# A two-layer chain on one core: front weights loaded in three parts, prepared weights with a due step, spread first loads, unchained output stores

## The chip, the cores and the metric

The kernel runs on one core of a Trainium2 chip. The metric is the device time of one execution in microseconds; before the change three runs took 874.82, 874.1 and 875.6 us, with a median of 874.82 us. Engines are named as in the profile: PE is TensorE (PEld its weight loads), DVE is VectorE, ACT is ScalarE, POOL is GpSimd, and SP is the engine that issues nearly all DMAs.

## The reference

Decayed attention of 4 x 8 heads feeds a gated layer and then a second layer with a piecewise quadratic gate. Weights come as 64-bit numbers, which the chip turns into float32.

```python
scores = q @ k^T / sqrt(64)              # (4, 8, 576, 576)
x = (scores * Dmat) @ v                  # Dmat[h, i, j] = gamma_h ** (i - j) for i >= j, else 0
x = x.transpose(0, 2, 1, 3).reshape(2304, 512)
xn = x / sqrt(mean(x * x) + 1e-6) * rms_g
x = (silu(xn @ w_gate) * (xn @ w_val)) @ w_out        # first layer, 512 -> 1536 -> 512
h = x @ w_in                                          # second layer, 512 -> 2048 -> 512
g = where(h >= 1, h, where(h <= -1, 0, (h + 1) ** 2 / 4))
out = g @ w_out2                                      # (2304, 512)
```

## The kernel before, in words

The 2304 tokens are worked in three batches of 768 (`NSB = 3`, `SB = 768`). After the attention comes the first layer: 36 steps (`step_a`, line 611), twelve for each batch, one for each 128 columns of the hidden size. Then comes the second layer: for each batch a front half (`x @ w_in`) and a back half (`g @ w_out2`).

Every product of 2 x 2 blocks is done with seven block products instead of eight, and every factor is kept as a high and a low part, so that one 128-row product is three matmuls (`three`, line 562). A front unit (`front_b`, line 735) is one of eight pairs of hidden columns of a batch. It has seven products of six matmuls, in the order 0, 1, 2, 3, 4, 6, 5. The loop at line 927 puts product number i of unit p at place 2i + 7p, so that a unit begins every seven places and two units alternate; the last place of a front half is 61. At places 56, 58 and 60 the first three pieces of the back half (`back_b`, line 814) stand between front products.

The weights of a front unit are prepared in the first layer. `prepare_b` (line 362) takes one of 16 units at the steps of `PREPARE` (line 43): eight for the front and eight for the back. It loads the 64-bit weights from `in_wb`, converts them (`convert`, line 284), makes sums (`wsum`), splits high from low into the one buffer `prep`, and stores 1792 KB to DRAM, to `wfd` for the front and `wod` for the back.

In the second layer unit q reads its weights from `wt0` or `wt1` (q even or odd). `load_wf` (line 701) loads them in two transfers: products 0 to 2 (768 KB) and products 3 to 6 (1024 KB). The first transfer for unit q + 2 is put after product 2 of unit q, when its place in the buffer is free, and the second after the last product of unit q.

`load_piece` (line 786) loads 512 KB of back weights from `wod` into a ring of six (`wback`). The ring shares its memory with `prep`. In batch 0 six of these loads are put at places 48 to 58 of the front half; afterwards each piece that is done loads one further on.

A result of the back half is added, transposed into a half of `o`, and stored by four DMAs of 96 KB (`store_out`, line 800). For the last result, which goes through a part of `plain`, two of the four are issued by ACT and two by SP.

What is written is not issued in that order. All engine calls go through `Plan` (line 46). `take` (line 98) records each with the earlier ones that it must follow, found from the overlap of the memory they touch; for DRAM that is the span from first to last element. `issue` (line 135) then works backwards through the list for a due time of each operation from costs of its own, and forwards for an order on every engine: of the operations that could start, the one due first. TensorE takes the first in the written order. So a due time sets how early an operation stands on VectorE, ScalarE and SP. `later_than` holds an operation back until a given one is done. On the chip each engine then runs its own list in order.

```python
for j, w, q in self.seen.get(name, []):            # take: who must come before
    over = r[0] < q[1] and q[0] < r[1] and r[2] < q[3] and q[2] < r[3]
    if over and (write or w or ...):
        before.add(j)
...
work = {2 * i + 7 * p: run for p in range(NPB) for i, run in enumerate(front_b(b * NPB + p))}
```

Of the kernel before, what the change touches and what calls it, by code (L numbers as in the profile page):

```python
# [36 lines left out]
EPS = 1e-6  # L37
WARM = 16
STAGE = 3
ATT = 6  # L40
FRONT, BACK = 0, 1
UNITS = [(p, kind) for p in range(NPB) for kind in (FRONT, BACK)]
# [3 lines left out]
class Plan:  # L46
# [8 lines left out]

    def __init__(self, nc):
        self.ops, self.seen, self.floor = [], {}, None
        for name in ("tensor", "vector", "scalar", "gpsimd", "sync"):
            setattr(self, name, Taker(self, name, getattr(nc, name)))

# [37 lines left out]
    def take(self, engine, real, method, args, kwargs):  # L98
        whole = lambda a: a[tuple(slice(None) for _ in a.shape)] if hasattr(a, "tag") else a
        args = [whole(a) for a in args]  # L100
        kwargs = {k: whole(a) for k, a in kwargs.items()}
        is_ap = lambda a: hasattr(a, "dep_tracking_offset")
        out = args[0] if args else kwargs["out"]
        ins = [a for k, a in kwargs.items() if k != "out" and is_ap(a)]
        if method == "matmul":
            ins = [kwargs["lhsT"], kwargs["rhs"]]
        i = len(self.ops)
        before = set()
        for ap, write in [(a, False) for a in ins] + [(out, True)]:
            name, *r = self.region(ap)  # L110
            kept = []
            for j, w, q in self.seen.get(name, []):
                over = r[0] < q[1] and q[0] < r[1] and r[2] < q[3] and q[2] < r[3]
                if over and (write or w or ap.space == PSUM and self.ops[j][0] != engine):
                    before.add(j)
                inside = r[0] <= q[0] and q[1] <= r[1] and r[2] <= q[2] and q[3] <= r[3]
                if not (write and inside):
                    kept.append((j, w, q))
            kept.append((i, write, r))
            self.seen[name] = kept  # L120
        if self.floor is not None and engine != "tensor":
            before.add(self.floor)
        before.discard(i)
        call = lambda: getattr(real, method)(*args, **kwargs)  # L124
        table = {ACTF.Silu: 1, ACTF.Abs_reciprocal_sqrt: 2}.get(kwargs.get("func"), 0)
        self.ops.append((engine, call, before, self.cost(engine, method, out, ins), method == "dma_start", table))

    @contextmanager
    def later_than(self, i):
# [2 lines left out]
        yield  # L132
        self.floor = None

    def issue(self):
        ops = self.ops
        n = len(ops)
        after = [[] for _ in range(n)]
        for i, o in enumerate(ops):
            for j in o[2]:  # L140
                after[j].append(i)

        def lag(j, i):
            if ops[j][0] == ops[i][0] and not ops[j][4]:
                return self.SAME.get(ops[j][0], 0)
            return self.PE_LATENCY if ops[j][0] == "tensor" else self.LATENCY

        due = [0.0] * n
        next_pe = None
        for i in reversed(range(n)):  # L150
            late = min((due[k] - lag(i, k) for k in after[i]), default=1e12)
            if ops[i][0] == "tensor":
                if next_pe is not None:
                    late = min(late, due[next_pe])
                next_pe = i
            due[i] = late - ops[i][3]
        wait = [len(o[2]) for o in ops]
        ready = [0.0] * n
        free = {}
        queue = {}  # L160
        rank = lambda i: i if ops[i][0] == "tensor" else due[i]
        for i in range(n):
            if not wait[i]:
                queue.setdefault(ops[i][0], []).append(i)
        dma_free, order, loaded = 0.0, [], 0
        while len(order) < n:
            best = None
            for e, q in queue.items():
                if not q:
                    continue  # L170
                t0 = max(free.get(e, 650.0), min(ready[i] for i in q))
                i = min((i for i in q if ready[i] <= t0 + self.HOLD), key=rank)
                start = max(free.get(e, 650.0), ready[i])
                if best is None or start < best[0]:
                    best = start, i
            start, i = best
            e, _, _, cost, dma, table = ops[i]
            if e == "scalar" and not dma and (table or not loaded) and table != loaded:
                cost, loaded = cost + 1283, table or 1
            if e == "tensor" and start < self.COLD:  # L180
                cost *= 2
            queue[e].remove(i)
            if dma:
                free[e] = start + 60
                dma_free = max(dma_free, start) + cost - 2000
                end = dma_free + 2000
            else:
                free[e] = end = start + cost
            order.append(i)
            for k in after[i]:  # L190
                wait[k] -= 1
                ready[k] = max(ready[k], end + lag(i, k))
                if not wait[k]:
                    queue.setdefault(ops[k][0], []).append(k)
        for i in order:
            ops[i][1]()
# [10 lines left out]
@with_exitstack  # L207
def moe_chain_kernel(ctx: ExitStack, tc: tile.TileContext, att, tail, wa, wb, dmat, gq, gk, out):
    nc = Plan(tc.nc)
    one = ctx.enter_context(tc.tile_pool(name="one", bufs=1))  # L210
    psum = ctx.enter_context(tc.tile_pool(name="psum", bufs=1, space=PSUM))
    dram = ctx.enter_context(tc.tile_pool(name="dram", bufs=1, space=DRAM))
# [354 lines left out]
    def product(w, j, ps, first, last):  # L567
        w = w.rearrange("p (j w k n) -> p j w k n", j=7, w=2, k=2)
        for k in range(2):
            three(  # L570
                ps, w[:, j, 0, k], w[:, j, 1, k], xs[:, j, 0, k], xs[:, j, 1, k], first and k == 0, last and k == 1,
                skip_group_check=True,
            )
# [33 lines left out]
        return [lambda d=d, wide=wide: part(d, wide) for wide in (False, True) for d in range(KD)]  # L607

    late = []

    def step_a(s):
        b, f = divmod(s, NA)
# [17 lines left out]
        w, h = wts[s % 2], hs[s % 2]  # L630
        d, x = front_banks(s)
        product(w, 0, d, True, False)
        after(0)
        if s < NA:
            with nc.later_than(len(nc.ops) - 1):
# [52 lines left out]
            sums_x()  # L688
        if s in PREPARE:
            limit[0] = len(slots)  # L690
            with nc.later_than(len(nc.ops) - 1):
                prepare_b()
        if s + 2 >= NA:
            if s + 2 < NSB * NA:
                load_a(s + 2, 1)
            else:
                for part in range(2):
                    load_wf(s + 2 - NSB * NA, part)


    def load_wf(q, part):
        if q < NSB * NPB:
            a, b = ((0, 3), (3, 7))[part]
            nc.sync.dma_start(
                out=wts[q % 2][:, a * 4 * P:b * 4 * P].bitcast(F32), in_=wfd[q % NPB][:, a * 4 * P:b * 4 * P]
            )
# [28 lines left out]
    def front_b(q):  # L735

        b, p = divmod(q, NPB)
        w = wts[q % 2]
# [15 lines left out]
        def after_4():  # L754
            nc.scalar.copy(out=u3, in_=d)
            nc.vector.tensor_add(out=g22, in0=x, in1=u3)
            gate_b(g22, g22)

        def after_6():
            gate_b(g12, d)  # L760

        def after_5():
            nc.vector.tensor_add(out=g21, in0=x, in1=u2)
            gate_b(g21, g21)
            load_wf(q + 2, 1)
            if p % 2:
                i = p // 2
                nc.vector.tensor_add(out=two(s1, i), in0=two(h21, i), in1=two(h22, i))
                nc.vector.tensor_sub(out=two(h21, i), in0=two(h11, i), in1=two(h21, i))
# [156 lines left out]
    for b in range(NSB):  # L926
        work = {2 * i + 7 * p: run for p in range(NPB) for i, run in enumerate(front_b(b * NPB + p))}
        end = max(work)
        for i, run in enumerate(held):
            work[2 * i + 1] = run  # L930
        back = back_b(b)
        for t in (end - 5, end - 3, end - 1):
            work[t] = back.pop(0)
        for t in sorted(work):
            if b == 0 and end - 14 <= t < end - 2 and t % 2 == 0:
                with nc.later_than(len(nc.ops) - 1):
                    load_piece()
            work[t]()
        if b + 1 < NSB:
            back, held = back[:-3], back[-3:]  # L940
        for i, run in enumerate(back):
            run()
            if i == NPB and b + 1 < NSB:
                with nc.later_than(len(nc.ops) - 1):
                    load_xb(b + 1)
# [63 lines left out]
```

## Time and profile before

| | before |
|---|---|
| median of three runs | 874.82 us (874.1 to 875.6) |
| profiled execution, its own time | 874.14 us |
| its span, first to last instruction | 872.4 us |
| PE busy | 850.5 us, 97% |
| DVE busy | 674.0 us, 77% |
| ACT busy | 565.0 us, 65% |
| granted TensorE clock, mean | 0.996 |
| DMA, mean over the span | 282 GB/s |

The shares are means over stages with different limits. Attention fills about the first 95 us, the first layer goes on to about 509 us, and the second layer fills the rest. The page has one line number for nearly all instructions, L124, because `Plan` makes every call there; so groups are told apart by what they write and read. `fr`, `acc` and `at` are PSUM banks, `xall` holds the tokens, `wt` the front weights, `rounded` the back weights, hidden values and the buffer `prep`, `o` the output. `att` and `plain` are shared by many temporaries. A releaser in brackets (`<-DMA wt<-wfd`) is what ended an idle time.

### The profile page before, as it was taken

Reading aid. Unit: us, or ns where it says so; the run is one execution under the profiler, and the core shown is the slowest. Engines: PE = TensorE matmul, PEld = TensorE weight load, DVE = VectorE, ACT = ScalarE, POOL = GpSimd, SP = SyncE. Lnnn points to the kernel's source line nnn. Section 1 sums busy time; section 2 is a strip of 40 time slices with the busy share of each in tenths; the row PEclk is TensorE's granted clock in tenths of the full one; section 3 lists DMA queues with packets and bytes.
Section 4 is the critical chain, followed back from the end, with each engine's and each line's share of the span. In section 5 each row is a group of like instructions: output and inputs, shape, how many; then the busy total and the mean of one; then the engine's idle time right before and its main releaser. Section 6 shows DMA issues by size and latency. Waiting matters only on the chain.

```text
span 872.4 us, 14665 instructions
## 1 busy us (share of the span) xinstructions
PE 850.5 (97%) x5460; PEld 811.9 (93%) x5460; DVE 674.0 (77%) x1077; ACT 565.0 (65%) x1019; POOL 52.1 (6%) x64
## 2 busy tenths in 40 slices
PE   8999899999999999999999999999999999999996
PEld 7987799999999999999999998999999999999996
DVE  3789888889988887979787876876767678567854
ACT  2647788887657767877666876745467646477541
POOL 3667000000000000000000000000000000000000
PEclk9999999999999999999999999999999999999999
DMA  9996788886868889699889879899886799784795
GB/s 355 338 354 208 233 276 271 286 276 203 263 234 309 326 291 367 219 333 392 301 283 353 304 283 348 280 356 318 257 263 253 262 282 319 257 273 151 205 272 127
DMA packets 116375, 246.03 MB, mean 282 GB/s; under 512 B 28240, under 2 KB 63312, under 8 KB 111184
## 3 DMA queue, kind: packets, MB, share of 16 engines
q1 hardware_dynamic: 114640, 243.69, 81.7%
q10 hardware_dynamic: 1664, 1.40, 0.5%
q8 instruction: 43, 0.70, 0.3%
q14 instruction: 28, 0.23, 0.1%
HBM read 185.82 MB, written 59.24 MB: 281 GB/s over the span
## 4 chain that ended last, share of the span: by engine, by line
PE 83%; DMA 11%; ACT 2%; DVE 2%; issue 1%; SPq 1%; POOL 0%; DVEq 0%; ACTq 0%
PE fr L124 37%; PE acc L124 30%; PE at L124 16%; DMA wt<-wfd 5%; DMA x1d<-plain 2%; DVE plain L124 1%; DMA rounded<-wod 1%; DMA plain<-in_wa_dram 1%; DMA xall<-x2d 1%; ACT xall L124 1%; SPq L124 1%; DMA plain<-in_dmat_dram 1%; ACT rounded L124 0%; DMA att<-in_att_dram 0%; DMA wt<-wfa 0%
## 5 line engine op out<-in xcount | busy, mean ns | idle before, releaser
L124 PE MATMUL fr<-xall,wt 128*128 128x384 f32 x2016 | 400.0, 337 | 1.8 <-ACT wt L124 0.6
L124 PEld LDWEIGHTS fr<-xall,wt 128*128 128x128 f32 x2016 | 353.7, 188 | 20.8 <-ACT att L124 2.9
L124 PE MATMUL acc<-rounded 128*128 128x384 f32 (+1 forms) x1224 | 275.6, 356 | 2.7 <-ACT att L124 1.3
L124 PEld LDWEIGHTS acc<-rounded 128*128 128x128 f32 x1224 | 215.3, 188 | 10.0 <-ACT att L124 2.4
L124 DVE TENSOR_TENSOR rounded<-plain,rounded 128x768 fp32r<-128x768 f32 (+1 forms) x96 | 88.4, 924 | 40.2 <-ACT rounded L124 39.9
L124 ACT CAST rounded<-plain 128x768 fp32r<-128x768 f32 (+1 forms) x96 | 77.6, 810 | 60.7 <-PE acc L124 33.9
L124 PE MATMUL at<-rounded 128*128 128x256 f32 (+1 forms) x648 | 111.4, 299 | 1.4 <-ACT rounded L124 1.3
L124 ACT COPY att<-fr 128x384 f32<-128x384 f32 x144 | 68.8, 478 | 57.7 <-PE fr L124 56.2
L124 ACT ACTIVATE att<-att 128x384 f32<-128x384 f32 x168 | 86.4, 524 | 24.4 <-DVE att L124 23.2
L124 DVE TENSOR_TENSOR att<-fr,att 128x384 f32<-128x384 f32 x144 | 78.7, 555 | 30.2 <-PE fr L124 18.8
L124 PEld LDWEIGHTS at<-rounded 128*128 128x128 f32 x648 | 98.4, 188 | 1.9 <-ACT rounded L124 1.6
L124 DVE TENSOR_TENSOR plain<-plain 128x768 f32<-128x768 f32 (+1 forms) x88 | 72.0, 831 | 0.6
L124 DVE SCALAR_TENSOR_TENSOR plain<-att,plain 128x384 f32<-128x384 f32 x72 | 39.1, 552 | 29.2 <-ACT att L124 29.2
L124 ACT ACTIVATE att<-plain 128x384 f32<-128x384 f32 x72 | 37.9, 526 | 36.2 <-DVE plain L124 36.1
L124 DVE TENSOR_TENSOR wt<-wt 128x768 fp32r<-128x768 f32 (+1 forms) x48 | 52.1, 1088 | 10.7 <-ACT wt L124 10.0
L124 PE MATMUL acc<-xall,wt 128*128 128x384 f32 x288 | 57.9, 335 | 0.6 <-ACT att L124 0.6
L124 ACT CAST wt<-wt 128x768 fp32r<-128x768 f32 (+1 forms) x48 | 45.3, 943 | 10.8 <-DMA wt<-wfa 10.4
L124 PEld LDWEIGHTS acc<-xall,wt 128*128 128x128 f32 x288 | 50.5, 188 | 1.1 <-ACT att L124 0.9
L124 ACT ACTIVATE plain<-plain,half 128x512 uint32<-128x512 uint8 x68 | 51.5, 765 | 0.0
L124 PE MATMUL at<-xall,wt 128*128 128x384 f32 x216 | 43.8, 337 | 2.7 <-DMA wt<-wfd 2.6
L124 ACT CAST rounded<-att 128x384 fp32r<-128x384 f32 x72 | 36.3, 513 | 9.0 <-DVE att L124 9.0
L124 DVE TENSOR_TENSOR rounded<-att,rounded 128x384 fp32r<-128x384 f32 x72 | 39.2, 551 | 3.6 <-ACT rounded L124 3.3
(91 smaller groups left out, 812.8 us busy)
## 6 DMA issues: line engine op xcount, KB each, us to landing
rounded<-wod SPq DMA_DIRECT2D x84, 512.0 KB, 4.9
wt<-wfd SPq DMA_DIRECT2D x24, 1024.0 KB, 7.3
plain<-in_wa_dram SPq DMA_DIRECT2D x36, 512.0 KB, 5.0
wt<-wfd SPq DMA_DIRECT2D x24, 768.0 KB, 4.9
plain<-in_wb_dram SPq DMA_DIRECT2D x32, 512.0 KB, 6.8
wfd<-rounded SPq DMA_DIRECT2D x8, 1792.0 KB, 8.0
wod<-rounded SPq DMA_DIRECT2D x8, 1792.0 KB, 8.8
att<-in_att_dram SPq DMA_DIRECT2D x26, 512.0 KB, 6.5
```

Source lines behind the costliest of these rows:

```text
L124: call = lambda: getattr(real, method)(*args, **kwargs)
```

## The change

Four edits.

1. Each prepared unit is given a due time. The operations of a `prepare_b` at step s are noted (`wanted_by`), and at step s + 6 (`UNIT_STEPS`) they are made due no later than the last operation written then, which is a matmul of that step's first product (`due_now`). Until now they were due only by whoever reads the stored weights or needs the buffer next. The unit prepared last, at step 30, gets no such time, since there is no step 36.
2. `load_wf` has three parts instead of two: products 0 to 2 (768 KB), 3 and 4 (512 KB), 5 and 6 (512 KB). The second is put after product 4 of the unit that frees the buffer, the third after its last product.
3. The six loads of back weights in batch 0's front half are put at places 31, 36, 41, 46, 51 and 56 instead of 48 to 58.
4. `take` no longer looks for overlaps of writes to `out` (`apart`). The stores of one result cover spans of `out` that interleave, so each counted as following the one before, though they touch different rows.

```diff
@@ class Plan
         self.ops, self.seen, self.floor = [], {}, None
+        self.apart, self.wanted = None, {}
...
-            for j, w, q in self.seen.get(name, []):
+            for j, w, q in () if name == self.apart else self.seen.get(name, []):
...
+    @contextmanager
+    def wanted_by(self, got):
+
+        at = len(self.ops)
+        yield
+        got.append(range(at, len(self.ops)))
+
+    def due_now(self, got):
+
+        for part in got:
+            self.wanted.update((i, len(self.ops) - 1) for i in part)
+        got.clear()
+
...
             late = min((due[k] - lag(i, k) for k in after[i]), default=1e12)
+            if i in self.wanted:
+                late = min(late, due[self.wanted[i]])
...
     nc = Plan(tc.nc)
+    nc.apart = out.tensor.name
@@ step_a
         product(w, 0, d, True, False)
+        nc.due_now(units_b[s % UNIT_STEPS])
...
-            with nc.later_than(len(nc.ops) - 1):
+            with nc.later_than(len(nc.ops) - 1), nc.wanted_by(units_b[s % UNIT_STEPS]):
                 prepare_b()
...
-                for part in range(2):
+                for part in range(3):
                     load_wf(s + 2 - NSB * NA, part)
@@ load_wf, front_b
-            a, b = ((0, 3), (3, 7))[part]
+            a, b = ((0, 3), (3, 5), (5, 7))[part]
...
             nc.vector.tensor_add(out=g22, in0=x, in1=u3)
             gate_b(g22, g22)
+            load_wf(q + 2, 1)
...
             gate_b(g21, g21)
-            load_wf(q + 2, 1)
+            load_wf(q + 2, 2)
@@ the loop over places
-            if b == 0 and end - 14 <= t < end - 2 and t % 2 == 0:
+            if b == 0 and end - 32 <= t < end - 2 and (end - t) % 5 == 0:
                 with nc.later_than(len(nc.ops) - 1):
                     load_piece()
```

What this does to the order on the engines, at three places.

At the start of the second layer, SP's queue before. `wt0` and `wt1` are the two weight buffers; a transfer 1536 wide is the first of a unit, 2048 wide the second; `wfd` and `wod` on the left are stores of prepared weights, `x2d` stores of the first layer's result.

```order
L124 DMA wt0_64<-wfd_91 128x1536
L124 DMA x2d_94<-plain_80 128x2x256
L124 DMA wfd_91<-rounded_79 128x3584
L124 DMA x2d_94<-plain_80 128x2x256
L124 DMA wt1_65<-wfd_91 128x1536
L124 DMA wt0_64<-wfd_91 128x2048
L124 DMA x2d_94<-plain_80 128x512
L124 DMA wt0_64<-wfd_91 128x1536
L124 DMA wod_92<-rounded_79 128x3584
L124 DMA x2d_94<-plain_80 128x512
L124 DMA wt1_65<-wfd_91 128x2048
```

The same place of SP's queue now; the two later transfers of a unit are 1024 wide.

```order
L126 DMA wod_92<-rounded_79 128x3584
L126 DMA wt1_65<-wfd_91 128x1024
L126 DMA x2d_94<-plain_80 128x2x256
L126 DMA wt0_64<-wfd_91 128x1536
L126 DMA x2d_94<-plain_80 128x2x256
L126 DMA x2d_94<-plain_80 128x512
L126 DMA wt0_64<-wfd_91 128x1024
L126 DMA x2d_94<-plain_80 128x512
L126 DMA wt1_65<-wfd_91 128x1536
L126 DMA wt0_64<-wfd_91 128x1024
```

Two stores of prepared weights stood after the first transfer of unit 2 (the first row of before); now the last of them stands ahead of it (the fourth row). The unit's second transfer stands before, and its third after, the first transfer of unit 3.

TensorE in the units that follow, before (`fr` are the banks of even units, `acc3` and `at0` those of odd ones).

```order
L124 MATMUL fr1_88<-xall_63,wt0_64 128x384 x6
L124 MATMUL fr0_87<-xall_63,wt0_64 128x384 x6
L124 MATMUL fr1_88<-xall_63,wt0_64 128x384 x6
L124 MATMUL fr0_87<-xall_63,wt0_64 128x384 x6
L124 MATMUL at0_81<-xall_63,wt1_65 128x384 x6
L124 MATMUL acc3_86<-xall_63,wt1_65 128x384 x12
L124 MATMUL at0_81<-xall_63,wt1_65 128x384 x6
```

And now:

```order
L126 MATMUL at0_81<-xall_63,wt1_65 128x384 x6
L126 MATMUL fr1_88<-xall_63,wt0_64 128x384 x6
L126 MATMUL acc3_86<-xall_63,wt1_65 128x384 x6
L126 MATMUL fr0_87<-xall_63,wt0_64 128x384 x6
L126 MATMUL at0_81<-xall_63,wt1_65 128x384 x6
L126 MATMUL fr0_87<-xall_63,wt0_64 128x384 x6
L126 MATMUL acc3_86<-xall_63,wt1_65 128x384 x6
```

Before, four products of an even unit stood in a row, and then two of the odd one on the same bank, `acc3`; now the two units alternate.

Towards the end of batch 0's front half, SP's queue before (`rounded<-wod` are pieces of back weights).

```order
L124 DMA wt0_64<-wfd_91 128x1536
L124 DMA wt1_65<-wfd_91 128x2048
L124 DMA rounded_79<-wod_92 128x2x512 x2
L124 DMA wt1_65<-wfd_91 128x1536
L124 DMA wt0_64<-wfd_91 128x2048
L124 DMA rounded_79<-wod_92 128x2x512 x5
L124 DMA wt1_65<-wfd_91 128x2048
L124 DMA rounded_79<-wod_92 128x2x512 x9
```

And now:

```order
L126 DMA wt1_65<-wfd_91 128x1024
L126 DMA rounded_79<-wod_92 128x2x512 x2
L126 DMA wt0_64<-wfd_91 128x1024
L126 DMA wt1_65<-wfd_91 128x1536
L126 DMA wt0_64<-wfd_91 128x1024
L126 DMA wt1_65<-wfd_91 128x1024
L126 DMA rounded_79<-wod_92 128x2x512
L126 DMA wt0_64<-wfd_91 128x1536
L126 DMA wt1_65<-wfd_91 128x1024
L126 DMA rounded_79<-wod_92 128x2x512
L126 DMA wt0_64<-wfd_91 128x1024
L126 DMA wt1_65<-wfd_91 128x1536
```

Two pieces and then five stood close together, all but two of them behind a second transfer; now the first four stand apart, among the transfers of units 6 to 9.

The end of SP's queue before (`o` are earlier results, `plain` is the last one).

```order
L124 DMA rounded_79<-wod_92 128x2x512
L124 DMA out_0_dram<-o_68 32x12x64 x5
L124 DMA out_0_dram<-plain_80 32x12x64
L124 DMA out_0_dram<-o_68 32x12x64 x2
L124 DMA out_0_dram<-plain_80 32x12x64
```

And now:

```order
L126 DMA out_0_dram<-o_68 32x12x64 x4
L126 DMA rounded_79<-wod_92 128x2x512
L126 DMA out_0_dram<-o_68 32x12x64 x4
L126 DMA out_0_dram<-plain_80 32x12x64 x2
```

Two stores of an earlier result stood between the last two stores; now all four of that result stand ahead of both.

## Rows read from the trace of the kernel before

**Rows 1.** The page's head: span and instructions.

```profile
span 872.4 us, 14665 instructions
```

**Rows 2.** What TensorE waited for, 505 to 873 us: total us, times, longest.

```profile
PE at L124 <- DMA wt<-wfd: 2.6, 5, 0.8
PE acc L124 <- ACT att L124: 1.9, 3, 0.7
PE acc L124 <- DMA rounded<-wod: 1.3, 1, 1.3
PE fr L124 <- DMA wt<-wfd: 0.4, 1, 0.4
```

**Rows 3.** Windows: length, busy PE, PEld, DVE, ACT, POOL, clock, DMA share, GB/s.

```profile
100.00:450.00 350.00, 350.00 (x1994) 331.47 (x1995) 298.55 (x509) 258.47 (x461) 0.00 (x0) 1.00 0.83 288
564.00:578.00 14.00, 12.72 (x74) 12.39 (x73) 8.38 (x13) 7.03 (x12) 0.00 (x0) 1.00 1.00 367
657.00:668.00 11.00, 11.00 (x66) 11.00 (x65) 8.81 (x14) 8.14 (x18) 0.00 (x0) 1.00 0.67 250
```

**Rows 4.** Timeline of TensorE, 522 to 541 us: start, us, what [idle before].

```profile
522.71 1.21 PE L124 MATMUL at<-xall,wt 128*128 128x384 f32 x6
524.32 1.28 PE L124 MATMUL fr<-xall,wt 128*128 128x384 f32 x6 [0.41 <-DMA wt<-wfd]
...
536.03 1.33 PE L124 MATMUL at<-xall,wt 128*128 128x384 f32 x6 [0.78 <-DMA wt<-wfd]
...
538.98 1.31 PE L124 MATMUL acc<-xall,wt 128*128 128x384 f32 x6 [0.57 <-ACT att L124]
540.13 1.20 PE L124 MATMUL at<-xall,wt 128*128 128x384 f32 x6
```

**Rows 5.** Timeline of TensorE, 652 to 657 us, one of five such places.

```profile
652.00 1.21 PE L124 MATMUL fr<-xall,wt 128*128 128x384 f32 x6
654.04 1.28 PE L124 MATMUL at<-xall,wt 128*128 128x384 f32 x6 [0.84 <-DMA wt<-wfd]
655.16 1.20 PE L124 MATMUL fr<-xall,wt 128*128 128x384 f32 x6
656.20 1.20 PE L124 MATMUL acc<-xall,wt 128*128 128x384 f32 x6
```

**Rows 6.** Timeline of TensorE, 570 to 574 us.

```profile
570.48 1.21 PE L124 MATMUL at<-xall,wt 128*128 128x384 f32 x6
572.97 0.76 PE L124 MATMUL acc<-rounded 128*128 128x384 f32 x3 [1.28 <-DMA rounded<-wod]
573.56 0.68 PE L124 MATMUL at<-rounded 128*128 128x384 f32 x3
```

**Rows 7.** Timeline of SP, 523 to 536 us: its DMA issues.

```profile
523.27 0.42 SPq L124 DMA_DIRECT2D wod<-rounded  x1
...
524.27 7.92 SPq L124 DMA_DIRECT2D wt<-wfd  x3
```

**Rows 8.** DMA issues, 630 to 690 us: count, KB each, median us to landing.

```profile
wt<-wfd SPq DMA_DIRECT2D x7, 1024.0 KB, 7.2
```

**Rows 9.** DMA issues, 524.2 to 524.6 us: the one issue there.

```profile
wt<-wfd SPq DMA_DIRECT2D x1, 1024.0 KB, 11.7
```

**Rows 10.** Timeline of SP and ACT's queues, 866 to 873 us.

```profile
866.97 0.32 SPq L124 DMA_DIRECT2D out_dram<-plain  x1
866.98 1.04 ACTq L124 DMA_DIRECT2D out_dram<-plain  x2
867.33 1.24 SPq L124 DMA_DIRECT2D out_dram<-o  x2
868.61 1.15 SPq L124 DMA_DIRECT2D out_dram<-plain  x1
```

**Rows 11.** DMA issues, 838 to 873 us: count, KB each, median us to landing.

```profile
out_dram<-plain SPq DMA_DIRECT2D x2, 96.0 KB, 2.4
out_dram<-plain ACTq DMA_DIRECT2D x2, 96.0 KB, 2.8
```

More of the change, by code (lines that the diff above doesn't have):

```diff
@@ L39 @@
 STAGE = 3
+UNIT_STEPS = 6
 ATT = 6
@@ L609, in moe_chain_kernel @@
     late = []
+    units_b = [[] for _ in range(UNIT_STEPS)]
     def step_a(s):
```

## The prediction

> **What bounds the kernel now.** I read the page first, for the span [rows 1], then what TensorE waits for after 505 us [rows 2], then the windows [rows 3], and last the stretches in which TensorE stands. The windows show that from 100 to 450 us, which is nearly all of the first layer, TensorE is busy for 350.00 of 350 us; the list of its waits after 505 us, the second layer, is short. So TensorE is the bound, and all that a change of order can give back is the time in which it stands late. Its normal pace is in [rows 5]: from 655.16 to 656.20 us it does six matmuls, 1.04 us, or 0.1733 us each. I call "lost" what two starts lie apart beyond 0.1733 us per matmul between them; that is a little more than the idle time in brackets, since after a stall the pipeline has to fill again.
>
> The losses of the second layer, by place:
> - **Front weights, batch 0.** From 522.71 to 540.13 us 84 matmuls start (14.56 us at the pace), and 17.42 us go by: 2.86 us lost. The rows in brackets name the load of the front weights twice and, for the last, ScalarE [rows 4].
> - **Front weights, batches 1 and 2.** From 652.00 to 655.16 us there are 12 matmuls: 3.16 - 2.08 = 1.08 us lost [rows 5]. There are five such places; the other four, by the same arithmetic, lost 0.37, 0.47, 0.81 and 0.46. Together 3.19 us.
> - **First back pieces.** From 570.48 to 573.56 us there are 9 matmuls: 3.08 - 1.56 = 1.52 us, ended by a load of back weights [rows 6].
> - The waits of "PE acc" for ScalarE in [rows 2] are three; one of them is inside the 2.86 us, the two others stand in the back halves and no edit touches them.
> - **The end.** The last store is issued on SP at 868.61 us, behind two stores of an earlier result which were put after the first of the last four [rows 10].
>
> **The change, part by part.**
>
> *Three transfers instead of two.* A front unit is seven products of 1.04 us; place t of product i of unit p is 2i + 7p. Before, the second transfer (products 3 to 6, 1024 KB) can start only after the unit's last product, place 12, and unit q+2 wants product 3 at place 20: 7 places lie between, 7 x 1.04 = 7.28 us. Such a load takes 7.2 us in the median from issue to landing [rows 8]. That is no reserve at all, so whichever load is a little late stalls TensorE. Now products 3 and 4 are loaded once product 4 is done (place 8): 11 places, 11.4 us, for 512 KB; and products 5 and 6 after place 12, while the first of the two to run, product 6, comes at place 24: again 11 places. A load of half the bytes with 4 us more of lead should be on time at all five places of batches 1 and 2: **-3.19 us**. The 24 added DMAs are issued by SP, whose queue is mostly waiting for TensorE here; a DMA issue occupies it 0.42 us [rows 7], which the 11.4 us cover.
>
> *Prepared weights stored by a set step.* The latest store of prepared back weights (1792 KB) is issued at 523.27 us, and the front load issued right behind it at 524.27 lands 11.7 us later instead of 7.2 [rows 7, 9]; TensorE stands for it at 536.03. By the order of the changed program that store is ahead of unit 2's first load, and TensorE's order goes back to alternating two units, where before it had two products of one unit in a row on one bank (the wait for ScalarE at 538.98 [rows 4]). With the earlier loads this takes away the batch-0 loss: **-2.86 us**. What is moved costs VectorE and ScalarE nothing new in work, but it is now done inside the first layer. There VectorE is busy 298.55 of 350 us [rows 3], so it has 15% free, and no matmul was late on it. Bounds: 0, or for each of the 13 units from the fourth on (the ones that move) a stall of the longest wait of its kind, 0.7 us idle [rows 2] and 0.17 of refill, 11.3 us in all. I take 0 as nearest: the stretch as busy as this one shows 350.00 of 350.
>
> *Back's first loads spread out.* They were at places 48 to 58 of 61; in the stretch 564 to 578 the DMA engines are busy all the time, 1.00 at 367 GB/s [rows 3], and the piece needed at 571.5 us is late. Now they stand at 31 to 56, and the first four are issued by place 48. They go between front loads, in stretches like 657 to 668 us, where the engines are 0.67 busy [rows 3]. Six pieces of 0.5 MB, 3.1 MB over 26 places (27 us), add 117 GB/s to the 250 there: 367 GB/s, just what the queue has carried. So the wait for back weights goes, **-1.52 us**, but the front loads of those 27 us have less air. I give back one stall, of the middle size of the five: **+0.47 us**, bounds 0 and five times that.
>
> *Output stores not chained.* The planner no longer puts each store after the landing of the one before. In the first two batches it moves stores among loads that are early anyway: 0, covered by the five pieces of back weights that lie ahead of TensorE. If that cover were gone, four issues in a row hold SP 1.7 us. At the end the last store of SP is issued right behind the first, at 867.33 instead of 868.61. ScalarE's queue then ends last: its two issues fill 866.98 to 868.02 [rows 10] and land in 2.8 us where SP's take 2.4 [rows 11]. SP's saving is 1.28 us; against ScalarE's later and slower landing I take **-0.8 us**, bounds 0 and -1.3.
>
> **Sum.** 3.19 + 2.86 + 1.52 + 0.8 - 0.47 = 7.90 us off. The profiled execution took 874.14 us (span 872.4 [rows 1] and 1.7 around it), so 866.2; the median of the runs shown, 874.82, is 0.68 above it, so 866.9.
>
> The page "DMA: Bandwidth & Descriptors" of the Trainium skill, in its section Bandwidth, under Measured, speaks against the split: "Batch DMAs to ≥1 MiB for ≥75% of peak". In [rows 3] the engines carry 367 GB/s while most of what is queued are 512 KB pieces, so here the rule does not hold for loads that queue behind one another. By the rule the halved loads would lose what their lead gains, and the sum would be 866.9 + 3.19 = 870.1.
>
> **The rivals.**
> - *Slower: the moved preparation stalls the first layer.* VectorE and ScalarE run in a fixed order; an instruction of a prepared weight that stands earlier waits for its load, and the copy of a front product behind it then holds TensorE's bank. At 0.87 us for a moved unit, 10 of the 13 units must stall TensorE before the 7.90 us are used up; all 13 give 874.8 - 7.9 + 11.3 = 878.2. For it: VectorE is 85% busy there, and the order of TensorE in the last third of the layer changes. Against: nothing was late there in 350 us. Chance 0.06.
> - *The front weights stay late.* SP issues in order, so a new transfer can stand behind something that waits; the engines are also nearly full in batch 0. Then only back pieces and end are gained: 874.8 - 1.52 - 0.8 = 872.5. Against it: in the new order each middle transfer is ahead of the other unit's next first transfer. Chance 0.12.
> - *Each further transfer costs its fixed time in the queue.* The shortest landing of a store, 2.4 us [rows 11], bounds that time. Engines 0.67 busy leave 2.4 us free in a unit's 7.28, so even then a unit just fits and the stalls stay, with the back pieces squeezed: about 875 to 880. Against: 367 GB/s in halves [rows 3]. Chance 0.03.
> - *The new deadlines change little on the chip* (the order moves, the waits merely change names): 874 to 875. Chance 0.05.
>
> **How the numbers follow.** The forecast has 0.74: 866.9. What a measurement of this kernel can tell from no change is 0.2%, 1.7 us; so faster means under 873.1. The forecast's own ends: 865.9 with the 0.47 not spent and 1.3 at the end, or 865.2 with the 0.7 us that the lowest run shown lies under its median; and 868.8 with five such stalls. To reach 8 in 10 the range goes on to 872.0, towards the second rival and a partial first one. Faster: the forecast and nearly all of the second rival, 0.85. Same: the fourth rival and parts of the others, 0.07. Slower: 0.08.
>
> **What would show it.** In TensorE's waits after 505 us "wt<-wfd" and "rounded<-wod" should be gone or under 0.5 us in total, while two waits of 0.7 us for ScalarE stay. The longest landing of a front load after 515 us should be well under 11.7 us. From 100 to 450 us TensorE should still be busy 350 us. At the end SP's last issue should lie within 0.5 us of the first of the last four. The prediction is wrong if the first layer shows waits of TensorE for ScalarE or VectorE, or if the front loads are still named.

## The result, and the profile after

The changed kernel took 864.97 us in the median of four runs (862.5 to 866.71), the kernel before 874.46 us in four (871.25 to 875.6). The ratio is 0.9896, with a 95% interval from 0.9875 to 0.9916: 7 to 11 us, or about 1.0%, faster. The forecast was 866.9 us and faster; the median lies 0.2 us under the low end of the range, 865.2, which was worked out against a median of before of 874.82 (as a ratio that end is 0.989, and the measured 0.9896 lies inside).

The page of the changed kernel, its head and TensorE's line of busy time:

```profile
span 861.9 us, 14713 instructions
...
PE 847.6 (98%) x5460; PEld 812.0 (94%) x5460; DVE 672.9 (78%) x1077; ACT 565.5 (66%) x1019; POOL 53.0 (6%) x64
```

The work is the same, 5460 matmuls; the span is 10.5 us shorter than that of [rows 1]. What TensorE waited for from 505 us to the end, which answers to [rows 2]:

```profile
PE acc L126 <- ACT att L126: 0.9, 2, 0.5
```

The three rows that named loads, `wt<-wfd` twice and `rounded<-wod`, are gone, 4.3 us of idle time in all. What stays is the wait for ScalarE, now 0.9 us in two places instead of 1.9 in three; the third was the one of 0.57 us at 538.98 in [rows 4], in the middle of batch 0's late loads. The windows that answer to the first of [rows 3], and the rest of the first layer:

```profile
100.00:450.00 350.00, 349.61 (x1990) 330.19 (x1989) 301.16 (x515) 261.27 (x466) 0.00 (x0) 1.00 0.85 297
450.00:505.00 55.00, 55.00 (x317) 52.32 (x316) 46.41 (x79) 39.90 (x70) 0.00 (x0) 1.00 0.86 310
```

In the first layer TensorE is busy for 349.61 of 350 us where it was 350.00; VectorE and ScalarE do about 3 us more there, the preparation that used to spill into the second layer. The timeline of TensorE at the place of [rows 4], in the changed kernel:

```profile
521.47 1.20 PE L126 MATMUL at<-xall,wt 128*128 128x384 f32 x6
522.51 1.20 PE L126 MATMUL fr<-xall,wt 128*128 128x384 f32 x6
523.55 1.20 PE L126 MATMUL acc<-xall,wt 128*128 128x384 f32 x6
524.59 1.20 PE L126 MATMUL fr<-xall,wt 128*128 128x384 f32 x6
525.63 1.20 PE L126 MATMUL at<-xall,wt 128*128 128x384 f32 x6
```

The two units alternate, and every product begins 1.04 us after the one before: the normal pace, with nothing in brackets. The DMA issues from 630 to 690 us, for [rows 8]:

```profile
wt<-wfd SPq DMA_DIRECT2D x16, 512.0 KB, 4.8
wt<-wfd SPq DMA_DIRECT2D x7, 768.0 KB, 4.8
```

A 512 KB transfer lands in 4.8 us, where 1024 KB took 7.2. The end, the timeline of SP's and ScalarE's queues after 856 us, for [rows 10]:

```profile
857.48 0.83 SPq L126 DMA_DIRECT2D out_dram<-plain  x2
857.48 0.90 ACTq L126 DMA_DIRECT2D out_dram<-plain  x2
```

Four issues fill 0.9 us, with nothing between them.

For the comparisons below I cut each profiled execution at two points of TensorE's timeline: the start of the first `at<-xall` product (unit 1 of the second layer) and the end of the last matmul. Between them lies nearly the whole second layer; after them the end.

| profiled execution | first `fr<-xall` | unit 1 begins | last matmul ends | second layer | end |
|---|---|---|---|---|---|
| before | 80.5 | 512.3 | 865.7 | 353.4 | 6.6 |
| changed | 79.7 | 511.1 | 856.2 | 345.2 | 5.6 |

So the second layer gave 8.2 us and the end 1.0. The other 1.2 us lie ahead of unit 1, and 0.8 of these even ahead of the first layer, where no instruction moved. That part differs from run to run: the first `fr<-xall` began between 77.6 and 82.4 us in the executions profiled for this study. Times of whole runs therefore scatter by some us, and the second layer of a profile tells the variants apart better than their medians do.

### The profile page after: what moved, and what is told of

It reads as the page before. It is cut to its first block, busy times and chain, and to the rows that moved or that the text cites. A ratio compares the mean times of both kernels' runs of the same rounds, so it can differ in the third digit from the quotient of the medians.

```text
span 861.9 us, 14713 instructions
## 1 busy us (share of the span) xinstructions
PE 847.6 (98%) x5460; PEld 812.0 (94%) x5460; DVE 672.9 (78%) x1077; ACT 565.5 (66%) x1019; POOL 53.0 (6%) x64
## 4 chain that ended last, share of the span: by engine, by line
PE 88%; DMA 6%; DVE 2%; ACT 2%; issue 1%; SPq 0%; POOL 0%; DVEq 0%; ACTq 0%
PE fr L126 40%; PE acc L126 33%; PE at L126 16%; DMA att<-in_att_dram 2%; DVE plain L126 1%; DMA wt<-wfa 1%; DMA plain<-in_att_dram 1%; DMA plain<-in_wa_dram 1%; DMA x1d<-plain 1%; DMA xall<-x2d 1%; ACT xall L126 1%; DMA plain<-in_dmat_dram 1%; ACT plain L126 0%; SPq L126 0%; ACT rounded L126 0%
## 5 line engine op out<-in xcount | busy, mean ns | idle before, releaser
L126 ACT ACTIVATE plain<-plain 128x512 f32<-128x512 f32 (+1 forms) x45 | 27.7, 621 | 22.6 <-DVE plain L126 10.4
```

## Experiments

First each edit was taken back alone, beside the same runs of before.

**u2_two_transfers**: the front weights in two transfers again.

```diff
-                for part in range(3):
+                for part in range(2):
                     load_wf(s + 2 - NSB * NA, part)
...
-            a, b = ((0, 3), (3, 5), (5, 7))[part]
+            a, b = ((0, 3), (3, 7))[part]
...
-            load_wf(q + 2, 1)
...
-            load_wf(q + 2, 2)
+            load_wf(q + 2, 1)
```

> The changed kernel with the front weights again in two transfers (products 0 to 2, 3 to 6); the other three edits stay. Lead theory (a second transfer with 7.28 us of lead against a 7.2 us load is what stalls TensorE): the five stalls of batches 1 and 2 come back, 3.2 us, and some 0.6 of batch 0, so 3.5 to 4.5 us over the changed kernel, and TensorE's waits after 505 us again name wt<-wfd, about 2 us idle. Contention theory (the loads were late because stores of prepared weights, output stores and pieces stood around them, which the other edits move): under 1 us over the changed kernel, no stall in batches 1 and 2.

Measured: 870.9 us, ratio 0.9976 [0.9952, 1.0001]. That is no longer clear of no change. The second layer takes 351.8 us, 6.6 more than with three transfers, which is more than the 3.5 to 4.5 expected. TensorE's waits after 505 us:

```profile
PE fr L126 <- DMA wt<-wfd: 1.9, 4, 0.9
PE acc L126 <- ACT att L126: 1.9, 2, 1.2
PE at L126 <- DMA wt<-wfd: 0.8, 2, 0.5
PE fr L126 <- DVE plain L126: 0.5, 1, 0.5
```

The loads are named again, six times, in all three batches. The contention theory, by which the other edits had cleared the queue, is out: with all of them in place the stalls are back. What goes beyond the expectation are waits that it had left out: those for ScalarE are 1.0 us longer than in the changed kernel, and one of 0.5 us for VectorE is new.

**u1_no_due**: no due time for the prepared weights.

```diff
-        nc.due_now(units_b[s % UNIT_STEPS])
...
-            with nc.later_than(len(nc.ops) - 1), nc.wanted_by(units_b[s % UNIT_STEPS]):
+            with nc.later_than(len(nc.ops) - 1):
                 prepare_b()
```

> The changed kernel without the due time of the prepared weights; the other three edits stay. Lead theory: the middle and last transfers have 11.4 us of lead, which covers even the 11.7 us landing behind the 1792 KB store nearly, so 0 to 0.7 us over the changed kernel. Contention theory: the batch-0 loss of 2.2 us at 536 us comes back nearly whole. If the due time itself harms the first layer, this one is faster than the changed kernel by up to 1 us.

Measured: 866.8 us, ratio 0.9923 [0.9902, 0.9944]; second layer 345.5 us, 0.3 more than with it; no wait of TensorE for a load after 505 us. With the three transfers in place the due time is worth nothing that these runs can show: the median is 1.8 us above the changed kernel's, but the intervals overlap, and in the profile 2.4 us lie in the first layer, which took 433.7 us from the first `fr<-xall` to unit 1 and scatters between 431.3 and 434.9 in the kernels without a nearer due time.

**u3_pieces_late**: the first back pieces at places 48 to 58 again.

```diff
-            if b == 0 and end - 32 <= t < end - 2 and (end - t) % 5 == 0:
+            if b == 0 and end - 14 <= t < end - 2 and t % 2 == 0:
```

> The changed kernel with the six first loads of back weights again at places 48 to 58; the other edits stay. Prediction's step: the wait for rounded<-wod comes back, 1.5 us. Rival (the wait was a consequence of the late 1024 KB transfers in the same queue): under 0.3 us, no such wait.

Measured: 868.82 us, ratio 0.9942 [0.9923, 0.9962]; second layer 347.4 us, 2.2 more. The timeline of TensorE shows a wait for a back piece at the same stage as in [rows 6], and a longer one:

```profile
563.87 1.21 PE L126 MATMUL acc<-xall,wt 128*128 128x384 f32 x6
566.88 1.31 PE L126 MATMUL acc<-rounded 128*128 128x384 f32 x6 [1.80 <-DMA rounded<-wod]
```

Between these starts lie 3.01 us for six matmuls: 1.97 lost. So the wait is not a consequence of 1024 KB transfers in the same queue: there are none here. Its size does hang on what else is queued, as the runs below show with the pieces at the same places: 1.8 us in two waits in o2_three_only, but only 0.3 us in o1_due_only.

**u4_chained**: the output stores chained in the planner again (`nc.apart` left out).

```diff
-    nc.apart = out.tensor.name
```

> The changed kernel with the output stores chained again in the planner; the other edits stay. Prediction's step: only the end changes, 0.8 us (bounds 0 and 1.3) over the changed kernel, SP's last issue again behind two stores of an earlier result. Rival (stores among the front loads of batches 1 and 2 delayed those loads): 1.5 us or more, and waits for wt<-wfd at the batches' beginnings.

Measured: 867.1 us, ratio 0.9925 [0.9899, 0.9951]; second layer 345.3 us, as in the changed kernel, and the end 6.8 us instead of 5.6. Only the end changes, by 1.2 us in the profile.

Then edits alone, on the kernel before.

**o2_three_only**: the three transfers alone.

```diff
-                for part in range(2):
+                for part in range(3):
                     load_wf(s + 2 - NSB * NA, part)
...
-            a, b = ((0, 3), (3, 7))[part]
+            a, b = ((0, 3), (3, 5), (5, 7))[part]
...
+            load_wf(q + 2, 1)
...
-            load_wf(q + 2, 1)
+            load_wf(q + 2, 2)
```

> The kernel before with the three transfers alone. Lead theory: all front-weight losses of batches 1 and 2 go (3.2 us) and most of batch 0's 2.86, the wait for rounded<-wod and the end stay: 5.0 to 6.0 us under the kernel before, ratio 0.993 to 0.994, and wt<-wfd in TensorE's waits after 505 us under 0.5 us. Contention theory: batch 0's stall of 0.8 us idle behind the late wod store stays and the gain is 3.5 us or less.

Measured: 869.08 us, ratio 0.9926 [0.99, 0.9952]; second layer 347.7 us, 5.7 less than before, end 6.7. TensorE's waits after 505 us:

```profile
PE acc L124 <- DMA rounded<-wod: 1.8, 2, 1.3
PE acc L124 <- ACT att L124: 0.7, 1, 0.7
```

No wait for front weights is left, in batch 0 neither, though the store of prepared weights was not moved. SP issues it at 523.43 us, as before:

```profile
523.43 0.38 SPq L124 DMA_DIRECT2D wod<-rounded  x1
```

The next two 512 KB loads behind it, a third transfer issued at 524.38 us and a second one at 527.17, have these rows:

```profile
wt<-wfd SPq DMA_DIRECT2D x1, 512.0 KB, 10.3
wt<-wfd SPq DMA_DIRECT2D x1, 512.0 KB, 8.8
```

They land late behind the store, but within the new lead of 11.4 us, and TensorE does not wait. The lead theory's numbers hold, but for the ratio, which is a shade under the 0.993 expected.

**o1_due_only**: the due time alone (`wanted_by`, `due_now` and their use in `issue`, as in the change's diff).

```diff
+            if i in self.wanted:
+                late = min(late, due[self.wanted[i]])
...
+        nc.due_now(units_b[s % UNIT_STEPS])
```

> The kernel before with the due time of the prepared weights alone. Prediction's step gave it and the split together 2.86 us in batch 0. Lead theory: with two transfers the five stalls of batches 1 and 2 stay, and in batch 0 the earlier store takes away at most the 2.2 us around 536 us, so 0 to 2 us under the kernel before. Contention theory: 2.2 us or more. If the due time harms the first layer, it is slower than the kernel before by over 1 us, with TensorE's waits between 100 and 505 us.

Measured: 873.43 us, ratio 0.999 [0.9971, 1.0009]; second layer 352.5 us, 0.9 less than before. In batch 0 the timeline of TensorE shows one stall in place of the two of [rows 4]:

```profile
525.01 1.21 PE L126 MATMUL at<-xall,wt 128*128 128x384 f32 x6
527.93 1.30 PE L126 MATMUL fr<-xall,wt 128*128 128x384 f32 x6 [1.71 <-DMA wt<-wfd]
```

The due time by itself moved the stall and did not end it.

Then what it is about the three transfers that helps.

**late_three**: three transfers, the second written beside the third, so as to take away its earlier start.

```diff
             gate_b(g22, g22)
-            load_wf(q + 2, 1)
...
+            load_wf(q + 2, 1)
             load_wf(q + 2, 2)
```

> The changed kernel with the second transfer (products 3 and 4) issued with the third, after the unit's last product, as the 1024 KB transfer was before: three transfers, but without the earlier start. If the lead is what counts, the stalls of batches 1 and 2 come back at least in part: 2 to 3.5 us over the changed kernel, wt<-wfd in TensorE's waits after 505 us. If it is enough that products 3 and 4 come in a transfer of their own and need not wait for the bytes of 5 and 6 (512 KB land 1 to 2 us sooner than 1024), under 0.7 us over the changed kernel and no such waits.

Measured: 864.22 us, ratio 0.9892 [0.9859, 0.9925]; second layer 344.5 us. TensorE's waits after 505 us, all of them:

```profile
PE acc L126 <- ACT att L126: 0.4, 1, 0.4
```

This run does not answer its question, since the earlier start is still there. The edit moved the call and not the transfer: `Plan` gives SP the transfer that is due first as soon as its place in the buffer is free, and nothing held the second one back until the last product. SP's issues in one round of 7.28 us, in late_three (the 768 KB transfer, then the two of 512 KB):

```profile
640.16 0.32 SPq L126 DMA_DIRECT2D wt<-wfd  x1
641.20 0.32 SPq L126 DMA_DIRECT2D wt<-wfd  x1
644.32 0.32 SPq L126 DMA_DIRECT2D wt<-wfd  x1
```

The same round in the changed kernel:

```profile
638.94 0.32 SPq L126 DMA_DIRECT2D wt<-wfd  x1
639.98 0.32 SPq L126 DMA_DIRECT2D wt<-wfd  x1
643.10 0.32 SPq L126 DMA_DIRECT2D wt<-wfd  x1
```

In both, one 512 KB transfer follows the 768 KB by 1.04 us, after a unit's last product, and the other by 4.16 us, three products later. That is after product 4 of the other unit and before its products 6 and 5, so only the transfer of products 3 and 4 can stand there. Over the whole traces SP's DMAs and TensorE's matmuls stand in the same order in both kernels. So late_three is the changed kernel once more, apart from the order on ScalarE and VectorE, and one wait for ScalarE fewer. Whether half the bytes or the earlier start is what helps, no run shows.

**seven_transfers**: every product's weights in a transfer of 256 KB, at the same places.

```diff
-                for part in range(3):
+                for part in range(7):
                     load_wf(s + 2 - NSB * NA, part)
...
-            a, b = ((0, 3), (3, 5), (5, 7))[part]
+            a, b = part, part + 1
...
-            load_wf(q + 2, 0)
+            for part in (0, 1, 2):
+                load_wf(q + 2, part)
...
-            load_wf(q + 2, 1)
+            for part in (3, 4):
+                load_wf(q + 2, part)
...
-            load_wf(q + 2, 2)
+            for part in (6, 5):
+                load_wf(q + 2, part)
```

> The changed kernel with the weights of every product in a transfer of their own (256 KB, seven for a unit instead of three), issued at the same places. If a further transfer costs a fixed time of some 2 us in the queue, four more a unit take 8 us of a unit's 7.28 and the second layer grows by tens of us. If queued transfers cost nothing but SP's issue (0.4 us each), within 1 us of the changed kernel, TensorE's waits for wt<-wfd under 0.5 us.

Measured: 866.7 us, ratio 0.9912 [0.9886, 0.9939]; second layer 345.1 us, as in the changed kernel. From 630 to 690 us:

```profile
wt<-wfd SPq DMA_DIRECT2D x51, 256.0 KB, 3.1
```

Four more transfers a unit cost nothing that shows in the second layer; the median is 1.7 us above the changed kernel's, with intervals that overlap. They bring nothing either, since no wait for front weights was left.

**due_in_one_step** and **due_in_three_steps**: the due time one or three steps after the preparation instead of six.

```diff
-UNIT_STEPS = 6
+UNIT_STEPS = 1
```

> The changed kernel with the due time of the prepared weights one step later instead of six (the unit prepared at step 30 has one now too). Rival that ends slower (the prepared weights' instructions hold up the first layer): with so little room VectorE and ScalarE serve them first, and TensorE waits for ScalarE or VectorE between 100 and 505 us, 0.87 us a unit, up to 13 us over the changed kernel. Prediction's step (the first layer has 15% of VectorE free and takes it): under 1.5 us over the changed kernel, waits between 100 and 505 us under 1.5 us in all.

> The changed kernel with the due time of the prepared weights three steps later instead of six, between the changed kernel and due_in_one_step (first layer 464.7 us instead of 431.3). If what counts is the room for a unit's work on VectorE and ScalarE beside a step's own, three steps hold about two units prepared in that time and their work, and the first layer stays within 2 us of 431 to 435, total within 2 us of the changed kernel. If every earlier due time takes from the steps in proportion, a third to a half of the 33 us: 10 to 16 us over the changed kernel, waits of TensorE for ScalarE and VectorE between 100 and 505 us.

Measured: 898.32 us, ratio 1.0305 [1.026, 1.035], and 880.07 us, ratio 1.0081 [1.0053, 1.0109]. The second layer is as in the changed kernel (344.9 and 346.0 us). From the first `fr<-xall` to unit 1 it takes 464.7 and 448.6 us instead of 431.3: 33 and 17 us more. TensorE's waits from 100 to 505 us with one step:

```profile
PE fr L126 <- ACT att L126: 11.0, 13, 2.7
PE fr L126 <- DVE att L126: 7.9, 6, 3.2
PE at L126 <- ACT rounded L126: 1.8, 4, 0.5
```

So the slower rival's mechanism exists, and it is not a narrow one: three steps already lose half of the 33 us, about as the second theory of that run said. I had expected room there. With six steps the changed kernel has one such wait in the first layer, 0.4 us.

Last, the wait for ScalarE that no edit touches.

**turned_pieces**: in the last piece of back product 4 and the first of 5, one half of the columns after the other.

```diff
-            for f in range(2):
-                for m in range(2):
-                    multiply(j, i, h, w, f, m)
+            turn = (j, i) in ((4, NPB // 2 - 1), (5, 0))
+            for a, c in itertools.product(range(2), range(2)):
+                multiply(j, i, h, w, *((c, a) if turn else (a, c)))
```

> The changed kernel; in the last piece of back product 4 and the first of product 5 the two halves of the output columns are taken one after the other instead of in turn, so that ScalarE has six matmuls (1.04 us) instead of three to read a bank before it is added to again. Theory: the waits of acc for ScalarE (0.2 to 1.0 us lost in each batch) go, 1.0 to 1.8 us under the changed kernel, ratio to the kernel before about 0.988. Rival: the wait is for another read of ScalarE (the operands of the next piece) and stays.

Measured: 864.42 us, ratio 0.9908 [0.9873, 0.9944]; second layer 345.0 us. The theory holds in batch 2 alone, where a start late by 0.2 us is gone. In batches 0 and 1 the waits stay, 1.0 us in two. ScalarE's timeline at the first of them:

```profile
605.94 0.83 ACT L126 CAST rounded<-plain 128x768 fp32r<-128x768 f32 x1
606.68 0.83 ACT L126 CAST xall<-plain 128x768 fp32r<-128x768 f32 x1
607.41 0.84 ACT L126 COPY att<-acc 128x384 f32<-128x384 f32 x2
608.15 0.84 ACT L126 CAST rounded<-plain 128x768 fp32r<-128x768 f32 x1
```

ScalarE has no pause: the copies that free the banks stand behind casts of the next batch's tokens (`xall`).

**xb_early**: `turned_pieces`, and the next batch's tokens loaded four pieces earlier.

```diff
-            if i == NPB and b + 1 < NSB:
+            if i == NPB // 2 and b + 1 < NSB:
                 with nc.later_than(len(nc.ops) - 1):
                     load_xb(b + 1)
```

> The kernel of turned_pieces with the next batch's tokens loaded four back pieces earlier (after piece 4 instead of 8), so that ScalarE's casts of them are done before it has to read the banks between products 4 and 5. New theory: in batches 0 and 1 the wait of acc for ScalarE is for a copy that stands behind these casts; it goes, 1.0 to 1.5 us under the changed kernel, and the time from the first product of unit 1 to the last matmul falls from 345.2 to about 344 us. Rival: the tokens' loads now stand among the back weights right after the front half and the pieces come late, a wait for rounded<-wod instead.

Measured: 864.14 us, ratio 0.9883 [0.9851, 0.9916]; second layer 344.0 us. TensorE's waits after 505 us:

```profile
PE acc L126 <- DVE rounded L126: 0.2, 1, 0.2
```

The waits for ScalarE are gone, and the second layer is 1.2 us shorter than in the changed kernel, as expected. In the time of whole runs that is inside the scatter: 0.9883 against 0.9896, with intervals that overlap. It beats the kernel before clearly, the changed kernel only in this part of its profile.

## Why the prediction was right, and where it was off

**The bound and the place.** TensorE was the bound and its lateness in the second layer the whole gain to be had. That held: 8.2 us came from the second layer, 1.0 from the end, against 7.1 (3.19 + 2.86 + 1.52 - 0.47) and 0.8 in the sum.

**Three transfers, 3.19 us.** Right in size: no wait for front weights is left in batches 1 and 2, and taking the edit back brings them back. But the step gave two reasons, half the bytes and 4 us more of lead, and no run parts them: late_three was to do it and left the order as it was. What the landings allow is an estimate. Of the 18 transfers of 512 KB that the changed kernel issues after 515 us right behind a unit's last product, where late_three meant the second one to stand, 17 landed within 6.8 us, so half the bytes might nearly have done with the old lead of 7.28. Behind the store of 1792 KB in o2_three_only such transfers took 8.8 and 10.3 us; there the longer lead was needed by this estimate.

**Batch 0, 2.86 us, given to the due time and the split together.** The loss went. o2_three_only and u1_no_due show that the split alone takes it away, o1_due_only that the due time alone does not. The reading of [rows 9] was true as far as it went: the load behind the 1792 KB store landed 4.5 us later. But moving the store was not needed: in o2_three_only the two 512 KB transfers behind it were as late, 10.3 and 8.8 us, and their lead of 11.4 us covered that.

**Back pieces, 1.52 us.** Right: u3_pieces_late has the wait again, 1.97 us there, and no kernel with the loads at the new places has one. They are not as evenly spread as the section on the change says: SP issues the first two of the six together, at 538.26 and 538.74 us, and the next two at 548.04 and 552.20.

**The +0.47 given back for a fuller queue in batch 0.** It did not come; no front load was late there. This is nearly half of the 1.1 us by which the second layer gave more than the sum. Another 0.4 us are the two waits for ScalarE in the back halves, which the prediction left as they were. Before, from 600 to 740 us, they were

```profile
PE acc L124 <- ACT att L124: 1.3, 2, 0.7
```

and in the changed kernel 0.9 us. (The third wait for ScalarE in [rows 2] is inside the 2.86 us.) Why they shrank was not tried by itself; xb_early shows that such waits hang on where ScalarE's casts fall. The rest, some 0.2 us, has no row.

**The end, 0.8 us.** 1.0 in the two profiles, and 1.2 between u4_chained and the changed kernel. SP's last issue starts 0.4 us after its first, as expected.

**The moved preparation, taken at 0.** Nearly right at six steps, where 15% of VectorE was free. The prediction named any wait of TensorE for ScalarE in the first layer as a sign of being wrong; one came, of 0.4 us, where the kernel before had none. The price of a stalled unit, 0.87 us, was too small for a tighter due time: with one step the first layer lost 33 us, three times the bound of 11.3, in 23 listed waits, the longest 3.2 us and not 0.7. The free share of an engine did not say how much room a due time leaves.

**The rivals.** The slower one lies on the other side of UNIT_STEPS and not in this change. That front weights stay late is refuted by the waits, that a further transfer costs its fixed time in the queue by seven_transfers. The halved loads lost nothing that a wait or the second layer's 345.2 us shows, so the rule of the Trainium skill's page "DMA: Bandwidth & Descriptors" (section Bandwidth, under Measured) on batching to 1 MiB did not decide here.

## What to carry to other kernels

When a consumer needs a buffer piece by piece, and the load lands just about when its lead ends, cut the transfer where the consumer's need is cut. The next piece then has fewer bytes in front of it, and its load can start as soon as its own place is free; which of the two counted here stays open. Do that before clearing the queue of other traffic: it alone took away the stalls that I had put down to a store nearby. Where a planner orders the calls, look in the trace whether an edit moved the instruction that it was to move, before reading its time: late_three's did not. And a due time given to a planner for background work should be loose: three steps instead of six turned a gain of 1% into a loss of 0.8%.

## What the runs showed that I had not expected

A stall of TensorE can cost more than its own length. In due_in_one_step it stands 3.24 us for VectorE, and the next matmuls are slow:

```profile
225.26 5.96 PE L126 MATMUL fr<-xall,wt 128*128 128x384 f32 x24 [3.24 <-DVE att L126]
231.06 0.28 PE L126 MATMUL at<-rounded 128*128 128x256 f32 x1
```

24 matmuls take 5.80 us from 225.26 to 231.06 us instead of 4.16. The windows of that execution show the granted clock before and there:

```profile
216.00:221.00 5.00, 5.00 (x29) 4.57 (x28) 4.09 (x7) 3.26 (x5) 0.00 (x0) 1.00 1.00 330
225.20:231.10 5.90, 5.84 (x25) 5.84 (x26) 4.55 (x8) 4.14 (x8) 0.00 (x0) 0.72 0.57 199
```

The mean of 0.72 is a part at 1.2 GHz and the rest at 2.4 GHz; it adds 1.64 us to a stall of 3.24. The stalls that this change removed, 1.3 us idle at the longest, have no such row: the clock in [rows 3] is 1.00 right through the one of [rows 6].

The length of one stall does not decide it, though. In the same execution the clock also fell behind a stall of 1.38 us, and in u3_pieces_late it stayed up behind the one of 1.80 us; the stall, the window behind it, and the window from the end of the other one:

```profile
383.34 1.34 PE L126 MATMUL fr<-xall,wt 128*128 128x384 f32 x6 [1.38 <-ACT att L126]
385.60:388.90 3.30, 3.30 (x12) 3.11 (x10) 2.44 (x5) 2.91 (x5) 0.00 (x0) 0.50 0.87 353
566.80:576.00 9.20, 9.12 (x52) 9.12 (x53) 4.63 (x7) 4.14 (x8) 0.00 (x0) 1.00 0.97 350
```

0.50 is 1.2 GHz and 1.00 is 2.4 GHz. Behind the 1.38 us TensorE soon stood again, 0.57 us before 385.25; what makes the clock fall these runs do not settle.
